# Smaller first groups and later weight loads at the start of a two-branch transformer kernel

## The chip, the cores and the metric

The kernel runs on one core of one Trainium2 chip. The metric is device time in microseconds of the whole program, median of several executions. A profile takes one execution; its times start at the first instruction.

Engine names in the profile: PE is the matmul engine, PEld its weight loads, DVE is VectorE, ACT is ScalarE, POOL is GpSimd, whose queue issues the stores, and SP issues the loads.

## The reference, cut to what matters

```python
x = A_x                                    # (1, 2048, 1024) bf16
xn = _layernorm(x)
return x + _A_ref(xn, ...) + _B_ref(xn, B_w1, B_w2, B_w3, B_w4)

def _B_ref(x, w1, w2, w3, w4):             # ... cut: padding
    h = _gelu(_layernorm(x) @ w1)          # 1024 x 1024
    hs = shifted(h) @ w2                   # four column blocks, shifted by -1, +1, -2, +2 rows
    x1 = x + hs
    return x1 + _gelu(_layernorm(x1) @ w3) @ w4
```

Branch A is an attention over segments; it comes later in the kernel and is not touched. The change is in the first 100 of about 1680 us: `xn`, the second layernorm `xn2`, and `h = gelu(xn2 @ w1)`.

## The kernel before

The rows of x are taken in 16 tiles of 128. `phase0` normalises a tile, stores `xn`, and transposes it on PE in two forms: `xn` through a spread matrix for branch A (`hst`), and `xn2` through the identity (`xn2T`). `stage1` multiplies by w1, four tiles at a time. A scheduler then orders the instructions of each engine into a list, and each engine runs its own list in that order (an instruction that is ready waits behind one that is not).

```python
for n in range(NT):                                          # 16 tiles
    xt = ring.tile([P, D], BF16, tag="xt", bufs=8)
    xts.append(xt)
    nc.sync.dma_start(xt[:], x_v[:, n, :])
    if n == 3:
        nc.sync.dma_start(w1_sb[:], ...)                     # 2 MB
nc.sync.dma_start(w2_sb[:], ...)                             # 2 MB
for k in range(KT):
    nc.sync.dma_start(w3_sb[:, k, :], w3_v[:, k, :])         # 8 x 0.9 MB

def phase0(g):
    hst  = ring2.tile([P, KT, 528], BF16, tag="hst")
    xn2T = ring2.tile([P, KT, 512], BF16, tag="xn2T")
    for j in range(4):
        n = 4 * g + j
        # DVE: bn_stats x2, bn_aggr, small ops; POOL: rr = pow(...)      ... cut
        xn = ring.tile([P, D], BF16, tag="xn")               # the ring has 3 buffers
        nc.vector.tensor_scalar(xn[:], xt[:], ...)
        nc.gpsimd.dma_start(xn_v[:, n, :], xn[:])            # store of xn, 256 KB
        nc.scalar.activation(xn2[:], xt[:], ACTF.Identity, ...)
        # PE: 8 spread matmuls of xn -> hst, copied by DVE (1) and ACT (2)
        # PE: 8 transposes of xn2  -> xn2T, copied by DVE (1) and ACT (1)
    nc.gpsimd.dma_start(hT_d[...], hst[:])                   # 1 MB
    return xn2T

def stage1(g, xn2T):
    for co in range(KT):
        ps = psum.tile([P, 512], F32, tag="mm", bufs=4)
        for k in range(KT):
            nc.tensor.matmul(ps[:], w1_sb[:, k, co*P:(co+1)*P], xn2T[:, k, :], ...)
        nc.scalar.activation(hTB[...], ps[:], ACTF.Gelu_apprx_tanh)

prev = phase0(0)
for g in range(1, 4):
    cur = phase0(g)
    stage1(g - 1, prev)
    prev = cur
stage1(3, prev)
# phase 2 follows: h @ w2, tile by tile
```

Of the kernel before, what the change touches and what calls it, by code (L numbers as in the profile page):

```python
# [13 lines left out]
BF16 = mybir.dt.bfloat16  # L14
F32 = mybir.dt.float32
I32 = mybir.dt.int32
ALU = mybir.AluOpType
ACTF = mybir.ActivationFunctionType
# [3 lines left out]
P = 128  # L22
S = 2048
D = 1024
KT = D // P
# [37 lines left out]
def kernel(  # L63
# [16 lines left out]
    nc = tc.nc  # L80
# [13 lines left out]
    hT_d = tc.dram_tile([P, KT, TH], BF16, name="hT_scratch")  # L94
# [4 lines left out]
    def const_tile(name, arr):  # L99
        d = nc.inline_tensor(_bf(arr), name=name)  # L100
        t = cpool.tile(list(arr.shape), BF16, name=name + "_sb")
        nc.gpsimd.dma_start(t[:], d.ap())
        return t

    spread_np = np.zeros((P, 132), np.float32)
    for t in range(P):
        j, i = divmod(t, SEG)
# [3 lines left out]
    ident = const_tile("c_ident", np.eye(P, dtype=np.float32))  # L111
# [12 lines left out]
    xsum = cpool.tile([P, KT, NSEG], BF16)  # L124
# [46 lines left out]
    with ExitStack() as bctx:  # L171
        psum = bctx.enter_context(tc.tile_pool(name="psum", bufs=2, space=PSUM))
        rctx = bctx.enter_context(ExitStack())
        w3_pool = rctx.enter_context(tc.tile_pool(name="w3", bufs=1, side="right"))
        w3_sb = w3_pool.tile([P, KT, F], BF16)
        w3_v = B_w3.rearrange("(k p) n -> p k n", p=P)
        with ExitStack() as hctx:
            keep = hctx.enter_context(tc.tile_pool(name="keep12", bufs=1))
            hTB = keep.tile([P, KT, S + 4], BF16)
            w2_sb = keep.tile([P, KT, D], BF16)  # L180
# [3 lines left out]
            with ExitStack() as p0:  # L184
                big = p0.enter_context(tc.tile_pool(name="p0big", bufs=1))
                ring = p0.enter_context(tc.tile_pool(name="p0ring", bufs=3))
                ring2 = p0.enter_context(tc.tile_pool(name="p0ring2", bufs=2))
                w1_sb = big.tile([P, KT, D], BF16)
                xts = []
                for n in range(NT):  # L190
                    xt = ring.tile([P, D], BF16, tag="xt", bufs=8)
                    xts.append(xt)
                    nc.sync.dma_start(xt[:], x_v[:, n, :])
                    if n == 3:
                        nc.sync.dma_start(w1_sb[:], B_w1.rearrange("(k p) n -> p k n", p=P))
                nc.sync.dma_start(w2_sb[:], B_w2.rearrange("(k p) n -> p k n", p=P))
                for k in range(KT):
                    nc.sync.dma_start(w3_sb[:, k, :], w3_v[:, k, :])
                def phase0(g):
                    hst = ring2.tile([P, KT, 528], BF16, tag="hst")  # L200
                    xn2T = ring2.tile([P, KT, 512], BF16, tag="xn2T")
                    for j in range(4):
                        n = 4 * g + j
                        xt = xts[n]
                        st = ring.tile([P, 2, 6], F32, tag="st")
                        for c in range(2):
                            nc.vector.bn_stats(st[:, c, :], xt[:, c * 512:(c + 1) * 512])
                        mv = ring.tile([P, 2], F32, tag="mv")
                        nc.vector.bn_aggr(mv[:], st[:])
                        ab = ring.tile([P, 2], F32, tag="ab")  # L210
                        nc.vector.tensor_scalar(ab[:, 0:1], mv[:, 1:2], EPS, None, op0=ALU.add)
                        nc.vector.tensor_scalar(ab[:, 1:2], ab[:, 0:1], EPS, mv[:, 1:2], op0=ALU.mult, op1=ALU.add)
                        rr = ring.tile([P, 2], F32, tag="rr")
                        nc.gpsimd.tensor_tensor(rr[:], ab[:], neghalf[:], op=ALU.pow)
                        nm2 = ring.tile([P, 1], F32, tag="nm2")
                        nc.vector.tensor_scalar(nm2[:], mv[:, 0:1], rr[:, 1:2], -1.0, op0=ALU.mult, op1=ALU.mult)
                        xn = ring.tile([P, D], BF16, tag="xn")
                        nc.vector.tensor_scalar(xn[:], xt[:], mv[:, 0:1], rr[:, 0:1], op0=ALU.subtract, op1=ALU.mult)
                        nc.gpsimd.dma_start(xn_v[:, n, :], xn[:])
                        xn2 = ring.tile([P, D], BF16, tag="xn2")  # L220
                        nc.scalar.activation(xn2[:], xt[:], ACTF.Identity, bias=nm2[:], scale=rr[:, 1:2])
                        for ei, (k0, kn) in enumerate(((0, 3), (3, 3), (6, 2))):
                            ps = psum.tile([P, 3, 132], F32, tag="tr")
                            for k in range(kn):
                                nc.tensor.matmul(ps[:, k, :], xn[:, (k0 + k) * P:(k0 + k + 1) * P], spread[:], start=True, stop=True)
                            if ei == 0:
                                nc.vector.tensor_copy(hst[:, k0:k0 + kn, 132 * j:132 * (j + 1)], ps[:, 0:kn, :])
                            else:
                                nc.scalar.copy(hst[:, k0:k0 + kn, 132 * j:132 * (j + 1)], ps[:, 0:kn, :])
                        for k0 in (0, 4):  # L230
                            ps = psum.tile([P, 4, P], F32, tag="tr")
                            for k in range(4):
                                nc.tensor.matmul(ps[:, k, :], xn2[:, (k0 + k) * P:(k0 + k + 1) * P], ident[:], start=True, stop=True)
                            if k0 == 0:
                                nc.vector.tensor_copy(xn2T[:, k0:k0 + 4, j * P:(j + 1) * P], ps[:])
                            else:
                                nc.scalar.copy(xn2T[:, k0:k0 + 4, j * P:(j + 1) * P], ps[:])
                    nc.gpsimd.dma_start(hT_d[:, :, 7 + 528 * g:7 + 528 * (g + 1)], hst[:])
                    nc.gpsimd.tensor_copy(xsum[:, :, 16 * g:16 * (g + 1)], hst[:].rearrange("p k (s i) -> p k s i", i=33)[:, :, :, 0])
                    return xn2T  # L240

                def stage1(g, xn2T):
                    for co in range(KT):
                        ps = psum.tile([P, 512], F32, tag="mm", bufs=4)
                        for k in range(KT):
                            nc.tensor.matmul(ps[:], w1_sb[:, k, co * P:(co + 1) * P], xn2T[:, k, :], start=(k == 0), stop=(k == KT - 1))  # L246
                        nc.scalar.activation(hTB[:, co, 2 + g * 512:2 + (g + 1) * 512], ps[:], ACTF.Gelu_apprx_tanh)

                prev = phase0(0)
                for g in range(1, 4):  # L250
                    cur = phase0(g)
                    stage1(g - 1, prev)
                    prev = cur
                stage1(3, prev)

            xn3T_pool = rctx.enter_context(tc.tile_pool(name="xn3T", bufs=1, side="right"))
            xn3T = xn3T_pool.tile([P, KT, S], BF16)
            with ExitStack() as p2:
                ring = p2.enter_context(tc.tile_pool(name="p2ring", bufs=4))
                for n in range(NT):  # L260
# [4 lines left out]
                    for ch in range(2):  # L265
                        ps = psum.tile([P, 512], F32, tag="mm", bufs=4)
# [16 lines left out]
                    for k0 in (0, 4):  # L283
                        ps = psum.tile([P, 4, P], F32, tag="tr")
# [4 lines left out]
        with ExitStack() as p3:  # L289
# [7 lines left out]
            for tb in range(4):  # L297
                for f in range(FT):
                    ps = psum.tile([P, 512], F32, tag="mm", bufs=4)
# [11 lines left out]
                for j in range(4):  # L311
                    n = tb * 4 + j
                    R1 = ring.tile([P, D], F32, tag="R1")
                    nc.sync.dma_start(R1[:], R1_v[:, n, :])
                    xt = ring.tile([P, D], BF16, tag="xt")
# [3 lines left out]
                    for ch in range(2):  # L319
                        ps = psum.tile([P, 512], F32, tag="mm", bufs=4)  # L320
# [190 lines left out]
    with tc.If(cond > 0):  # L511
        with ExitStack() as fctx:
# [17 lines left out]
            with tc.For_i(0, NSEG, 1) as i:  # L530
                nc.sync.dma_start(hseg[:, :, M:L], hT_d[:, :, bass.ds(i * 33 + 8, SEG)])
                nc.sync.dma_start(Rt[M:L, :], R_d[bass.ds(i * SEG, SEG), :])
                for hg in range(8):
# [8 lines left out]
                    ps = fps.tile([P, 4, L], F32, tag="mm")  # L542
# [4 lines left out]
                    ps = fps.tile([P, 4, L], F32, tag="mm")  # L547
# [4 lines left out]
                    ps = fps.tile([P, 512], F32, tag="mm")  # L552
# [33 lines left out]
                for ch in range(2):  # L586
                    ps = fps.tile([P, 512], F32, tag="op")
# [47 lines left out]
```

## Time and profile before

1681.85 us, median of four executions (1681.47 to 1682.9).

| what | before | view |
|---|---|---|
| PE busy over the span | 97% | the page, part 1 |
| first stage1 matmul | 26.9 us | timeline |
| first phase 2 matmul | 99.4 us | timeline |
| DMA, 10 to 56 us | saturated, about 400 GB/s | table by stretches |

The busy times of the whole span, from the page:

```profile
PE 1634.8 (97%) x10385; PEld 856.5 (51%) x10385; DVE 647.7 (39%) x1528; ACT 641.8 (38%) x1305; POOL 221.5 (13%) x380
```

PE is the bottleneck nearly everywhere, so time can only be won where PE stands. That is at the start. The table by stretches gives busy microseconds of each engine (with the number of instructions), the granted PE clock (1.00 also where the trace has no clock record), and the busy share and rate of the DMA engines:

```profile
core 0: us, PE busy (x) PEld busy (x) DVE busy (x) ACT busy (x) POOL busy (x), PEclk, DMA share, GB/s
10.20:16.40 6.20, 2.77 (x20) 2.08 (x21) 4.58 (x15) 4.37 (x6) 2.53 (x5) 1.00 1.04 394
16.40:30.00 13.60, 10.05 (x66) 6.80 (x66) 12.16 (x35) 9.35 (x15) 6.49 (x10) 1.00 1.04 404
30.00:56.50 26.50, 23.31 (x175) 13.03 (x173) 21.60 (x64) 20.92 (x35) 10.42 (x16) 1.00 1.02 396
```

Between 16.4 and 30 us PE runs 66 matmuls only. The chain of waits (start, duration, what) shows stage1 starting on a slow PE, and one store of xn that took 13 us:

```profile
26.33 0.82 PE ps L225 x6
27.15 2.13 PE ps L246 x5
29.28 0.16 PE ps L225 x2
29.44 0.43 PE ps L246 x2
...
43.17 13.22 DMA xn_scratch<-xn
```

L246 is stage1, L225 the spread. The first five stage1 matmuls of 512 columns take 0.426 us each, two microseconds later they take 0.216. The timeline (start, duration, engine, line, operation, shapes, number) shows the end of the stage; L269 is phase 2:

```profile
77.40 22.18 PE L246 MATMUL ps<-xn2T,w_sb 128*128 128x512 bf16 x102
99.42 8.15 PE L269 MATMUL ps<-w_sb,hTB 128*128 128x512 bf16 x37
```

Phase 2 follows without a gap. So what the change is worth is read from the start of phase 2.

**PE's busy time is not its work.** Matmuls overlap, and an isolated one shows as longer (a matmul of 512 columns shows as 0.379 us on the average of the profile page, but in a long row one starts every 0.216 us), so below I count work instead: a matmul of N columns counts as N / 2.4 GHz + 2.5 ns. The Trainium skill, "TensorE: Matmul & The Clock Gate", Part 1, gives this as the start-to-start time on a warm PE; this trace agrees (102 matmuls of 512 columns from 77.40 to 99.42 us are 0.216 us each). Stage1 and phase0 together need about 70 us of it. What the clock shows beyond that is *lost* PE time. In the kernel before it is 24.1 us by 30 us (10.2 of them before the first matmul) and 5.0 us more by 70 us. Sums hold to about half a microsecond, since some matmul records are missing from a trace.

### The profile page before, as it was taken

To read this page: it belongs to the slowest core of one execution; us is meant where nothing else is said; L and a number is where in the kernel's file an instruction comes from. 1 tells how busy PE (TensorE), PEld (TensorE's weight loads), DVE (VectorE), ACT (ScalarE), POOL (GpSimd) and SP (SyncE) were. 2 spreads that over 40 slices of the span, in tenths; PEclk is the share of its full clock that TensorE was granted. 3 is DMA by queue.
4 is the path that set the end of the run, shared out by engine and by line. 5 is a ranking of instruction groups with operands and counts; after the bars stand their busy time and mean duration, and the time that the engine had idled before them with its cause. 6 is when DMAs were issued, how large, how long until landed. Compare 5 with 4: busy or idle time off the path is not lost.

```text
span 1679.1 us, 26722 instructions
## 1 busy us (share of the span) xinstructions
PE 1634.8 (97%) x10385; PEld 856.5 (51%) x10385; DVE 647.7 (39%) x1528; ACT 641.8 (38%) x1305; POOL 221.5 (13%) x380
## 2 busy tenths in 40 slices
PE   5999999999999999999999999999999999999998
PEld 3544444444445455554555545554555546665643
DVE  7447000000101145553455505564255533465540
ACT  6635402112030045551455405553255514565520
POOL 4222011010200122210111101110011100101000
PEclk9999999999999999999999999999999999999999
DMA  9544522030309888553556526664365533445211
GB/s 357 225 169 171 188 63 63 31 95 1 100 26 315 313 277 264 169 161 93 171 182 193 165 82 191 181 184 146 116 192 173 179 97 120 137 129 152 65 45 45
DMA packets 202803, 252.93 MB, mean 151 GB/s; under 512 B 15691, under 2 KB 165400, under 8 KB 202672
## 3 DMA queue, kind: packets, MB, share of 16 engines
q1 hardware_dynamic: 186928, 217.25, 41.1%
q0 software_dynamic: 15744, 33.92, 5.8%
q8 instruction: 84, 1.38, 0.4%
q14 instruction: 47, 0.39, 0.1%
HBM read 204.11 MB, written 30.07 MB: 139 GB/s over the span
## 4 chain that ended last, share of the span: by engine, by line
PE 74%; DVE 11%; ACT 5%; DMA 5%; issue 4%; POOL 0%; SPq 0%; DVEq 0%; ACTq 0%; POOLq 0%
PE ps L403 16%; PE ps L415 13%; PE ps L301 11%; PE ps L346 11%; PE ps L322 11%; DVE Pn L463 3%; DVE ss L459 3%; PE psT L467 2%; PE psO L473 2%; ACT e L457 2%; PE psS L450 2%; DVE sm L455 2%; DVE sm L452 2%; DMA wv<-in_A_Wv_dram 1%; PE ps L246 1%
## 5 line engine op out<-in xcount | busy, mean ns | idle before, releaser
L403 PE MATMUL ps<-hTb,wk 128*128 128x396 bf16 (+2 forms) x1536 | 265.7, 313 | 0.0
L403 PE MATMUL ps<-hTb,wq 128*128 128x396 bf16 (+2 forms) x1536 | 263.6, 314 | 0.8 <-DVE Ro L323 0.8
L428 POOL DMA_DIRECT2D V<-Vp x240 | 118.5, 500 | 881.4 <-ACT Vp L416 878.4
L346 PE MATMUL ps<-wo_sb,oX 128*128 128x512 bf16 x1024 | 228.9, 379 | 0.0
L415 PE MATMUL ps<-wv,xTb 128*128 128x512 bf16 x1024 | 227.7, 379 | 0.0
L322 PE MATMUL ps<-w_sb,h3T 128*128 128x512 bf16 x896 | 197.1, 379 | 0.0
L301 PE MATMUL ps<-xn3T,w_sb 128*128 128x512 bf16 x896 | 194.4, 379 | 0.0
L407 ACT ACTIVATE QT<-ps 128x396 bf16<-128x396 f32 (+2 forms) x192 | 87.6, 466 | 255.6 <-PE ps L403 255.6
L452 DVE TENSOR_TENSOR sm<-psS,c_mask_reg_sb 99x396 f32<-99x396 f32 x160 | 87.4, 564 | 217.9 <-PE psS L450 217.9
L403 PEld LDWEIGHTS <-wq 128*128 128x128 bf16 x1536 | 133.6, 98 | 71.3 <-issue 1.1
L302 ACT ACTIVATE h3T<-ps 128x512 bf16<-128x512 f32 x112 | 66.8, 598 | 268.1 <-PE ps L301 268.1
L403 PEld LDWEIGHTS <-wk 128*128 128x128 bf16 x1536 | 131.4, 98 | 67.5
L415 PEld LDWEIGHTS <-xTb 128*128 128x128 bf16 x1024 | 99.8, 98 | 115.8
L346 PEld LDWEIGHTS <-oX 128*128 128x128 bf16 x1024 | 97.8, 98 | 112.2 <-DVE oX L476 1.6
L301 PEld LDWEIGHTS <-w_sb 128*128 128x128 bf16 x896 | 87.6, 98 | 105.2
L322 PEld LDWEIGHTS <-h3T 128*128 128x128 bf16 x896 | 86.9, 98 | 103.1
L323 DVE TENSOR_TENSOR Ro<-ps,R 128x512 f32<-128x512 f32 x32 | 22.1, 691 | 295.6 <-PE ps L322 295.5
L416 ACT CAST Vp<-ps 128x512 bf16<-128x512 f32 x128 | 75.1, 587 | 151.2 <-PE ps L415 147.8
L469 ACT CAST PT<-psT 99x396 bf16<-99x396 f32 (+1 forms) x176 | 86.1, 489 | 62.1 <-PE psT L467 61.1
L405 ACT CAST KT<-ps 128x396 bf16<-128x396 f32 (+2 forms) x192 | 87.7, 457 | 49.1 <-PE ps L403 49.0
L459 DVE TENSOR_REDUCE ss<-e 99x4 f32<-99x396 f32 (+1 forms) x176 | 95.0, 545 | 24.5 <-ACT e L457 23.3
L463 DVE TENSOR_TENSOR Pn<-e,rs 99x396 bf16<-99x396 f32 (+1 forms) x176 | 97.6, 559 | 6.6
(110 smaller groups left out, 1455.3 us busy)
## 6 DMA issues: line engine op xcount, KB each, us to landing
wv<-in_A_Wv_dram SPq DMA_DIRECT2D x48, 1024.0 KB
wq<-in_A_Wq_dram SPq DMA_DIRECT2D x40, 1024.0 KB
wk<-in_A_Wk_dram SPq DMA_DIRECT2D x40, 1024.0 KB
V<-Vp SPq DMA_DIRECT2D x272, 32.0 KB
xt<-in_A_x_dram SPq DMA_DIRECT2D x32, 256.0 KB
R_scratch<-x POOLq DMA_DIRECT2D x16, 512.0 KB, 3.9
R<-R_scratch SPq DMA_DIRECT2D x16, 512.0 KB
R_scratch<-Ro POOLq DMA_DIRECT2D x16, 512.0 KB, 5.0
```

Of the source, the lines that this page charges most:

```text
L301: nc.tensor.matmul(ps[:], w3_sb[:, k, f * P:(f + 1) * P], xn3T[:, k, tb * 512:(tb + 1) * 512], start=(k == 0), stop=(k == KT - 1))
L322: nc.tensor.matmul(ps[:], h3T[:, f, j * P:(j + 1) * P], w4_sb[:, f, ch * 512:(ch + 1) * 512], start=(f == 0), stop=(f == FT - 1))
L346: nc.tensor.matmul(ps[:], oX[:, h, gl * P:(gl + 1) * P], wo_sb[:, h, cc], start=(h == 0), stop=(h == H - 1))
L403: nc.tensor.matmul(ps[:, :nb], w[:, k, hh * P:(hh + 1) * P], B["hTb"][:, k, :nb], start=(k == 0), stop=(k == KT - 1))
L405: nc.scalar.copy(dst[:, hh, :nb], ps[:, :nb])
L407: nc.scalar.mul(dst[:, hh, :nb], ps[:, :nb], scale)
L415: nc.tensor.matmul(ps[:], B["xTb"][:, k, m * P:(m + 1) * P], wv[:, k, :], start=(k == 0), stop=(k == KT - 1))
L428: eng.dma_start(V[r0:r0 + SEG, ti, :], Vp[SEG * (sl % 4):SEG * (sl % 4 + 1), sl // 4, :])
L452: nc.vector.tensor_tensor(sm[:T, :, :T], S3, msk[:].unsqueeze(1).to_broadcast((T, 4, T)), op=ALU.add)
L459: nc.vector.tensor_reduce(ss[:T, :], e[:T, :, :T], axis=AX.X, op=ALU.add)
L463: nc.vector.tensor_tensor(Pn[:T, :, :T], e[:T, :, :T], rs[:T, :].unsqueeze(2).to_broadcast((T, 4, T)), op=ALU.mult)
L469: nc.scalar.copy(PT[:T, :, :T], T3)
```

## The change

Its intent: let stage1 start after one tile rather than four, and keep the 9 MB of w2 and w3, not needed until 100 us and later, out of the way of the loads and stores that the start waits for. It also puts the transposes of xn2 ahead of the spread matmuls.

```diff
-                nc.sync.dma_start(w2_sb[:], ...)
-                for k in range(KT):
-                    nc.sync.dma_start(w3_sb[:, k, :], w3_v[:, k, :])
-                def phase0(g):
-                    xn2T = ring2.tile([P, KT, 512], BF16, tag="xn2T")
-                    for j in range(4):
-                        n = 4 * g + j
+                def phase0(n0, nt):
+                    xn2T = ring2.tile([P, KT, 512], BF16, tag="xn2T", bufs=3)
+                    for jj in range(nt):
+                        n = n0 + jj
 ... (hst is still one buffer for four tiles, stored after the fourth)
-                        nc.scalar.activation(xn2[:], xt[:], ACTF.Identity, ...)
+                        a_xn2 = nc.scalar.activation(xn2[:], xt[:], ACTF.Identity, ...)
+                        if n == 13:
+                            late = [nc.sync.dma_start(w2_sb[:], ...)]
+                            late += [nc.sync.dma_start(w3_sb[:, k, :], ...) for k in range(KT)]
+                            for d in late:
+                                tc.add_manual_dep(d.ins, a_xn2.ins.name, ...)
+                        # transposes of xn2 now first, then the spread matmuls (moved block)
 ...
-                def stage1(g, xn2T):
+                def stage1(n0, nt, xn2T):
+                    w = nt * P
-                            nc.tensor.matmul(ps[:], ..., xn2T[:, k, :], ...)
+                            nc.tensor.matmul(ps[:, :w], ..., xn2T[:, k, :w], ...)
 ...
+                for nt in (1, 1, 2, 4, 4, 4):
+                    groups.append((n0, nt)); n0 += nt
+                # phase0 of a group, then stage1 of the group before it, as before
```

More of the change, by code (lines that the diff above doesn't have):

```diff
@@ L195 @@
                         nc.sync.dma_start(w1_sb[:], B_w1.rearrange("(k p) n -> p k n", p=P))
-                nc.sync.dma_start(w2_sb[:], B_w2.rearrange("(k p) n -> p k n", p=P))
-                for k in range(KT):
-                    nc.sync.dma_start(w3_sb[:, k, :], w3_v[:, k, :])
-                def phase0(g):
-                    hst = ring2.tile([P, KT, 528], BF16, tag="hst")
-                    xn2T = ring2.tile([P, KT, 512], BF16, tag="xn2T")
-                    for j in range(4):
-                        n = 4 * g + j
+                hst_cur = [None]
+                def phase0(n0, nt):
+                    xn2T = ring2.tile([P, KT, 512], BF16, tag="xn2T", bufs=3)
+                    for jj in range(nt):
+                        n = n0 + jj
+                        g, j = divmod(n, 4)
+                        if j == 0:
+                            hst_cur[0] = ring2.tile([P, KT, 528], BF16, tag="hst", name="hst")
+                        hst = hst_cur[0]
                         xt = xts[n]
@@ L220, in phase0 @@
                         xn2 = ring.tile([P, D], BF16, tag="xn2")
-                        nc.scalar.activation(xn2[:], xt[:], ACTF.Identity, bias=nm2[:], scale=rr[:, 1:2])
+                        a_xn2 = nc.scalar.activation(xn2[:], xt[:], ACTF.Identity, bias=nm2[:], scale=rr[:, 1:2])
+                        if n == 13:
+                            late = [nc.sync.dma_start(w2_sb[:], B_w2.rearrange("(k p) n -> p k n", p=P))]
+                            late += [nc.sync.dma_start(w3_sb[:, k, :], w3_v[:, k, :]) for k in range(KT)]
+                            for d in late:
+                                tc.add_manual_dep(d.ins, a_xn2.ins.name, mybir.DependencyInfo(mybir.DependencyClass.Sync, mybir.DependencyReason.DATA),
+                                                  reason="delay bulk weight loads")
+                        for k0 in (0, 4):
+                            ps = psum.tile([P, 4, P], F32, tag="tr")
+                            for k in range(4):
+                                nc.tensor.matmul(ps[:, k, :], xn2[:, (k0 + k) * P:(k0 + k + 1) * P], ident[:], start=True, stop=True)
+                            if k0 == 0:
+                                nc.vector.tensor_copy(xn2T[:, k0:k0 + 4, jj * P:(jj + 1) * P], ps[:])
+                            else:
+                                nc.scalar.copy(xn2T[:, k0:k0 + 4, jj * P:(jj + 1) * P], ps[:])
                         for ei, (k0, kn) in enumerate(((0, 3), (3, 3), (6, 2))):
@@ L229, in phase0 @@
                                 nc.scalar.copy(hst[:, k0:k0 + kn, 132 * j:132 * (j + 1)], ps[:, 0:kn, :])
-                        for k0 in (0, 4):
-                            ps = psum.tile([P, 4, P], F32, tag="tr")
-                            for k in range(4):
-                                nc.tensor.matmul(ps[:, k, :], xn2[:, (k0 + k) * P:(k0 + k + 1) * P], ident[:], start=True, stop=True)
-                            if k0 == 0:
-                                nc.vector.tensor_copy(xn2T[:, k0:k0 + 4, j * P:(j + 1) * P], ps[:])
-                            else:
-                                nc.scalar.copy(xn2T[:, k0:k0 + 4, j * P:(j + 1) * P], ps[:])
-                    nc.gpsimd.dma_start(hT_d[:, :, 7 + 528 * g:7 + 528 * (g + 1)], hst[:])
-                    nc.gpsimd.tensor_copy(xsum[:, :, 16 * g:16 * (g + 1)], hst[:].rearrange("p k (s i) -> p k s i", i=33)[:, :, :, 0])
-                    return xn2T
-                def stage1(g, xn2T):
+                        if j == 3:
+                            nc.gpsimd.dma_start(hT_d[:, :, 7 + 528 * g:7 + 528 * (g + 1)], hst[:])
+                            nc.gpsimd.tensor_copy(xsum[:, :, 16 * g:16 * (g + 1)], hst[:].rearrange("p k (s i) -> p k s i", i=33)[:, :, :, 0])
+                    return xn2T
+                def stage1(n0, nt, xn2T):
+                    w = nt * P
                     for co in range(KT):
@@ L245, in stage1 @@
                         for k in range(KT):
-                            nc.tensor.matmul(ps[:], w1_sb[:, k, co * P:(co + 1) * P], xn2T[:, k, :], start=(k == 0), stop=(k == KT - 1))
-                        nc.scalar.activation(hTB[:, co, 2 + g * 512:2 + (g + 1) * 512], ps[:], ACTF.Gelu_apprx_tanh)
-                prev = phase0(0)
-                for g in range(1, 4):
-                    cur = phase0(g)
-                    stage1(g - 1, prev)
+                            nc.tensor.matmul(ps[:, :w], w1_sb[:, k, co * P:(co + 1) * P], xn2T[:, k, :w], start=(k == 0), stop=(k == KT - 1))
+                        nc.scalar.activation(hTB[:, co, 2 + n0 * P:2 + n0 * P + w], ps[:, :w], ACTF.Gelu_apprx_tanh)
+                groups = []
+                n0 = 0
+                for nt in (1, 1, 2, 4, 4, 4):
+                    groups.append((n0, nt))
+                    n0 += nt
+                prev = None
+                for (n0, nt) in groups:
+                    cur = (n0, nt, phase0(n0, nt))
+                    if prev is not None:
+                        stage1(*prev)
                     prev = cur
-                stage1(3, prev)
+                stage1(*prev)
             xn3T_pool = rctx.enter_context(tc.tile_pool(name="xn3T", bufs=1, side="right"))
```

## The prediction

> **What bounds the kernel now.** The page gives PE 97% busy over 1679.1 us; TensorE works nearly everywhere but at the start, and the change touches only that start (phase0 + stage1). In the timeline stage1's last matmul ends at about 99.4 us and phase 2 follows without a gap, so the gain is how much earlier that moment comes.
>
> Until then PE needs 256 matmuls of 128x512 (102 of them run in 22.0 us, 0.216 us each: 55 us) and 16 tiles of transposes and spreads (in the chain about 0.43 + 0.47 us a tile: 14.5 us), 70 us in all. It takes 99, so about 29 us are lost before 60 us: 10.2 us before the first matmul; 10.2 to 26.9 us, where there are only transposes (VectorE paces a tile at 3.2 us); 26.9 to 41.4 and 47.5 to 59.8 us, where ScalarE, VectorE or late xn stores hold the tiles back. From 59.8 us PE is bound by its own work (36 matmuls, four tiles with 26 between them, then a tail of 102). DMA is saturated (about 400 GB/s) from 5 to 50 us; one xn store took 13.2 us, which with three xn buffers alone allows a tile every 4.4 us.
>
> **What the change does.** w2 and w3 (2 + 7 MB) leave the first 45 us, so that x loads and xn stores get the bandwidth. Groups of 1, 1, 2, 4, 4, 4 tiles let stage1 start at about 12.5 us, once w1 has landed, rather than at 26.9. Matmuls of 128 columns are free on a warm PE: the transposes of 128 columns run at 54 ns, a quarter of 216. The Trainium skill, "TensorE: Matmul & The Clock Gate", Part 1, says that PE runs at half clock until it has been busy for about 3.4 us; the trace agrees (stage1's first matmuls take 0.426 us each, later 0.216), and denser early work should end this by about 20 us instead of 29. The cost is on ScalarE: 16 gelus of 128 columns (estimate 0.25 us) and 8 of 256 (0.38) in place of 8 of 512 (0.60), +2.2 us.
>
> **How much counts.** In the changed order PE has 153 matmuls and four tiles left after tile 11: 33.0 + 3.6 = 36.6 us. Before it had 164, from 59.8 us. Up to tile 11's last copy ScalarE's order holds 15 xn2 (1.2), 12 xn2T (0.55), 12 hst pairs (0.76), 16 + 8 + 4 gelus and one table load (1.28): 44 us, from 9.7 us. At full density tile 11 would be done at 54 us, at 92% (it had about 94% at 27 to 41 us) at 58. So stage1 ends at 58 + 36.6 = 94.5 us, 5 us sooner; VectorE is nearly as full. PE stops being starved, but ScalarE then binds, so only a fifth of the idle time is won. Later stages keep their pace.
>
> **Prediction.** 1677.0 us, 8 in 10 within 1672.5 to 1680.5. Faster by over 2%: 0.005; within 2%: 0.99; slower: 0.005.
>
> **What would show it.** Timeline: first stage1 matmul at 12 to 14 us; PE warm by 20 us; xn stores landing in about 6 us until w2/w3 start at about 48 us; ScalarE about 90% busy from 15 to 57 us; stage1's last matmul near 94.5 us; phase 2 keeping 4.15 us a tile; no wait for w2 or w3.
>
> **What would make it wrong.** If ScalarE and VectorE interlock badly (below 85% density) the gain shrinks to nothing. If their waits vanish, it is up to 10 us. The 9 MB now collide with the last tiles' xn stores, and could stall tiles 14 and 15 for some us. If w1 lands late, PE, which runs in order, blocks in front of it with tile 1 behind.

## The result, and the profile after

1675.71 us, median of 8 runs (1673.51 to 1676.76), against 1681.85 for the kernel before (12 runs). The ratio is 0.9962, 95% interval 0.9952 to 0.9971. (A ratio is the mean time of one kernel's fast runs over that of the other's in the same rounds, so not quite the ratio of the medians. The record lists two more executions of the changed kernel, the profiled one at 1675.5 and one at 1677.35, outside these eight.) The change saves about 6 us. The predicted time was 1677.0 in 1672.5 to 1680.5, so the number was right.

The busy times and the table by stretches after the change:

```profile
PE 1632.0 (98%) x10513; PEld 862.6 (52%) x10513; DVE 646.9 (39%) x1528; ACT 640.6 (38%) x1321; POOL 221.1 (13%) x380
```

```profile
core 0: us, PE busy (x) PEld busy (x) DVE busy (x) ACT busy (x) POOL busy (x), PEclk, DMA share, GB/s
10.20:16.40 6.20, 1.04 (x9) 0.88 (x10) 3.97 (x14) 3.46 (x4) 2.50 (x5) 1.00 1.05 396
16.40:30.00 13.60, 13.39 (x186) 12.64 (x186) 12.46 (x37) 12.76 (x30) 4.61 (x7) 1.00 0.51 178
30.00:56.50 26.50, 24.72 (x233) 17.40 (x231) 23.39 (x67) 23.78 (x47) 13.00 (x21) 1.00 0.60 193
```

Between 16.4 and 30 us PE now runs 186 matmuls (most of them small) where it ran 66, and the DMA engines are half idle. Before 16.4 us it does less than it did. Why is seen in the timeline; L233 is the transposes of xn2, L209 bn_stats, L235 the VectorE half of the copy to xn2T, L241 the spread, L256 stage1:

```profile
10.98 1.03 PE L233 MATMUL ps<-c_ident_sb,xn 128*128 128x128 bf16 x8 [10.98 <-ACT xn L223]
...
13.61 0.69 DVE L209 BATCH_NORM_STATS2 st<-xt 128x6 f32<-128x512 bf16 x1 [2.23 <-DMA xt<-in_A_x_dram]
...
15.67 0.67 DVE L235 CAST xn2T<-ps 128x512 bf16<-128x512 f32 x1
...
16.39 0.49 PE L241 MATMUL ps<-c_spread_sb,xn 128*128 128x132 bf16 x3 [4.38 <-DVE xn2T L235]
...
16.68 0.74 PE L256 MATMUL ps<-xn2T,w_sb 128*128 128x128 bf16 x5
...
17.87 1.81 PE L256 MATMUL ps<-xn2T,w_sb 128*128 128x128 bf16 x15
...
20.43 0.82 PE L256 MATMUL ps<-xn2T,w_sb 128*128 128x128 bf16 x11
```

The transposes of tile 0 are done at about 12 us, but the copy that hands them on stands in VectorE's list behind the statistics of tile 4, whose load queues behind w1. PE waits 4.38 us for it. From 17.87 us fifteen matmuls of 128 columns take 0.107 us each (half clock); from 20.43 us they soon run at 0.056.

```profile
71.88 22.18 PE L256 MATMUL ps<-xn2T,w_sb 128*128 128x512 bf16 x102
93.89 8.15 PE L285 MATMUL ps<-w_sb,hTB 128*128 128x512 bf16 x37
```

Phase 2 (now L285) starts at 93.9 us, 5.5 us sooner; the span is 5.4 us shorter (1679.1 to 1673.7), so in these two traces the later stages neither add nor take.

### The profile page after: what moved, and what is told of

It reads as the page before. It is cut to its first block, busy times and chain, and to the rows that moved or that the text cites. A ratio compares the mean times of both kernels' runs of the same rounds, so it can differ in the third digit from the quotient of the medians.

```text
span 1673.7 us, 26997 instructions
## 1 busy us (share of the span) xinstructions
PE 1632.0 (98%) x10513; PEld 862.6 (52%) x10513; DVE 646.9 (39%) x1528; ACT 640.6 (38%) x1321; POOL 221.1 (13%) x380
## 4 chain that ended last, share of the span: by engine, by line
PE 75%; DVE 10%; ACT 5%; DMA 4%; issue 2%; POOL 0%; SPq 0%; DVEq 0%; ACTq 0%; POOLq 0%
PE ps L419 16%; PE ps L431 13%; PE ps L317 12%; PE ps L362 11%; PE ps L338 11%; DVE Pn L479 3%; DVE ss L475 2%; PE psT L483 2%; PE psO L489 2%; PE ps L256 2%; ACT e L473 2%; PE psS L466 2%; DMA wv<-in_A_Wv_dram 1%; DVE sm L471 1%; DVE sm L468 1%
```

## The experiments

Twelve kernels ran, in three groups of four, each group on one chip beside the kernel before. Every one gave a correct result. The table has for each the time and ratio (where it was timed in rounds), the start of phase 2 from its trace, and lost PE time up to 30 us and from there to 70 us, counted as above.

| kernel | us (runs) | ratio to before | phase 2 starts | lost by 30 us | lost 30 to 70 us |
|---|---|---|---|---|---|
| before | 1681.85 (12) | | 99.4 | 24.1 | 5.0 |
| changed | 1675.71 (8) | 0.9962 | 93.9 | 19.2 | 4.8 |
| delay alone | 1681.98 (5) | 0.9994 | 100.0 | 24.5 | 5.0 |
| groups alone | 1680.98 (5) | 0.9996 | 100.2 | 19.4 | 10.2 |
| groups alone, 6 xn buffers | 1675.47 (5) | 0.9969 | 94.3 | 19.6 | 5.4 |
| before, 6 xn buffers | 1680.86 (1) | | 100.2 | 25.1 | 6.1 |
| changed, more ScalarE work | 1678.33 (1) | | 94.3 | 20.0 | 4.2 |
| changed, more VectorE work | 1675.00 (1) | | 92.2 | 18.8 | 3.8 |
| changed, more PE work | 1680.78 (1) | | 98.9 | 19.3 | 4.5 |
| changed, old transpose order | 1674.30 (5) | 0.9957 | 92.3 | 18.7 | 3.5 |
| changed, x before w1 | 1676.51 (5) | 0.9969 | 94.3 | 19.2 | 4.9 |
| changed, tile 0 copied by ScalarE | 1675.70 (5) | 0.9968 | 93.7 | 20.4 | 3.3 |
| old order, tile 0 copied by ScalarE | 1673.96 (5) | 0.9956 | 92.7 | 19.4 | 3.2 |
| old order, tile 0 by ScalarE, w1 after two tiles | 1678.66 (5) | 0.9990 | 95.4 | 21.5 | 4.4 |

The intervals of the ratios are about plus or minus 0.0014 (2.4 us), so the differences of one or two microseconds between the versions at 1674 to 1676.5 us are not resolved by the times. The trace of the single run with more ScalarE work has a lower mean clock (0.997 against 1.0 for the changed kernel), so its total of 1678.33 is not used; only its start is.

The clock records inside the traces, which no view above prints, show one source of this scatter. In the traces of nine of the twelve kernels PE drops to half clock once or twice more after the start, for 3.41 us each time, at 112 to 120 us or at 627 to 635 us; in those of the kernel before and the changed kernel it does not. Each drop is worth at most 1.7 us (an estimate: half of 3.41). The records also say when PE first leaves half clock: at 29.24 us in the kernel before, 20.51 in the changed one, and up to 3.5 us later in variants of either. A later one costs about half of the delay, so starts of phase 2 that differ by about a microsecond are not told apart by one trace each.

### The two halves of the change, one at a time

The delay alone, with groups of four and the old order:

```diff
-                for nt in (1, 1, 2, 4, 4, 4):
+                for nt in (4, 4, 4, 4):
 # and bufs=3 of xn2T taken back, spread matmuls first again
```

> The kernel before with one part of the change: w2 and w3 issued after the ScalarE pass of tile 13; groups of 4 tiles and the old order of transposes stay. Theory A (late xn stores behind 9 MB of weights held tiles 8 to 11 back, and ScalarE/VectorE bind elsewhere): stage1 ends about 2 us sooner than 99.4 us. Rival B (the gain is the bandwidth alone): about 5 us sooner, near 94. Rival C (the gain is the small groups alone): no change, 99.4.

Measured: phase 2 starts at 100.0 us, the ratio is 0.9994 (interval 0.9981 to 1.0008). No gain. The stores of xn did get fast (median 3.3 us to landing, 6.0 before), and nothing came of it (PE leaves half clock 1.4 us later than in the kernel before, which by the estimate above would account for the 0.6 us). Theory A is wrong about this kernel.

The groups alone, with w2 and w3 issued early again:

```diff
-                        if n == 13:
-                            late = ...
+                nc.sync.dma_start(w2_sb[:], ...)          # ahead of phase0, as before
+                for k in range(KT):
+                    nc.sync.dma_start(w3_sb[:, k, :], w3_v[:, k, :])
```

> The changed kernel with w2 and w3 issued early as before. Theory A: the small groups fill PE from 16 us on, so most of the gain stays: stage1 ends at 95 to 97 us, between the two kernels. Rival B (bandwidth alone): 99. Rival C (groups alone): 94.

Measured: phase 2 starts at 100.2 us, ratio 0.9996 (0.9982 to 1.001). No gain either, so all three theories failed: each half alone is worth nothing, both together 6 us. The table shows how. The groups alone do win the first 30 us (19.4 us lost, as in the changed kernel, not 24.1), and lose them again later (10.2 us, not 4.8). The chain of waits of this run shows where; L223 writes xn, L232 copies to xn2T, L253 is stage1:

```profile
45.95 12.84 DMA xn_scratch<-xn
...
58.88 0.55 DVE xn L223
...
59.55 0.61 DVE xn2T L232
...
61.59 6.74 PE ps L253 x24
```

VectorE waits for a free xn buffer until a store, issued at 45.95 us amid the weights, has landed (the store of tile 10, whose buffer tile 13 needs). It stood 4.78 us for it, and PE 4.05 us. Then comes a second cost, in the table by stretches of the same run:

```profile
58.00:60.00 2.00, 0.00 (x0) 0.00 (x0) 1.12 (x3) 0.00 (x0) 0.27 (x1) 1.00 0.54 220
60.00:62.00 2.00, 1.79 (x13) 1.11 (x13) 1.09 (x3) 0.86 (x3) 0.31 (x1) 0.80 0.37 145
62.00:64.00 2.00, 2.00 (x7) 0.64 (x5) 0.18 (x1) 0.51 (x2) 1.70 (x3) 0.50 0.12 46
64.00:66.00 2.00, 2.00 (x9) 0.83 (x8) 0.00 (x0) 0.60 (x1) 0.05 (x1) 0.84 1.00 348
```

The granted clock falls to 0.50, by the clock records from 61.21 to 64.63 us. The 24 matmuls took 6.74 us in place of 24 x 0.216 = 5.18. This is what "TensorE: Matmul & The Clock Gate", Part 1, of the Trainium skill says: PE goes back to half clock after an idle window of about 3.4 us and needs as long of work to leave it. So the stand of 4 us cost 5.6.

### Is it the bandwidth, or three buffers?

If the weights hurt by holding xn buffers, more buffers should do what the delay does, with the weights left early.

```diff
-                        xn = ring.tile([P, D], BF16, tag="xn")
+                        xn = ring.tile([P, D], BF16, tag="xn", bufs=6)
```

> The small groups with w2 and w3 early, as in the run without the delay, but with six xn buffers rather than three. Theory (the early weights cost their 6 us because VectorE waits for an xn buffer whose store takes 13 us): the wait goes and stage1 ends at 94 to 96 us instead of 100, about 1676 us. Rival (the bandwidth itself is short: x loads and hT stores are late too): 98 to 100, no gain.

Measured: phase 2 at 94.3 us, 1675.47 us, ratio 0.9969 (0.9955 to 0.9982). The stores are no faster: a median of 6.6 us to landing, 6.8 with three buffers. The start of phase 2 (L282) with three buffers, with six, and the view of the stores with six:

```profile
100.17 6.21 PE L282 MATMUL ps<-w_sb,hTB 128*128 128x512 bf16 x28
94.28 1.89 PE L282 MATMUL ps<-w_sb,hTB 128*128 128x512 bf16 x8
DMA to landing us min/median/max: 5.7/6.6/13.5
```

but no instruction waits for them, and the loss after 30 us is 5.4 us, not 10.2. One word in the kernel does what the manual delay of nine loads does. The rival, that bandwidth itself was short, is out.

The same edit on the kernel before:

> The kernel before with six xn buffers. The claim in the prediction that late xn stores held its tiles back says stage1 ends 1 to 3 us sooner than 99.4. Rival (in the kernel before the tiles are early enough, the front is what costs): no change within 0.7 us.

Measured: phase 2 at 100.2 us, no gain. (This is one trace, and PE leaves half clock at 32.08 us in it, 2.8 us later than in the kernel before, so the start of phase 2 alone would not exclude a gain below a microsecond.) The waits say the same more surely: in the trace of the kernel before, VectorE waited 0.2 us in all for a store, in the groups-alone run 6.7 (1.9 before tile 10, 4.8 before tile 13). So in the kernel before, the stores held almost nothing: with groups of four PE falls behind in the first 30 us, and by the time tile 13 is wanted, 56.49 us, its buffer has just come free. The two limits lie one behind the other. Removing the later one shows nothing until the earlier one is gone, and removing the earlier one only brings the work to the later one.

### What binds in the changed kernel after 20 us?

The prediction says ScalarE. ScalarE and VectorE are both busy some 90% from 30 to 56.5 us. To tell, each engine got more work, tiles 0 to 11, with the result unused:

```diff
+                        if n < 12:                          # ScalarE run
+                            junk = ring.tile([P, 512], BF16, tag="junk")
+                            nc.scalar.copy(junk[:], xn2[:, 0:512])
```

```diff
+                        if n < 12:                          # VectorE run
+                            junk = ring.tile([P, 6], F32, tag="junk")
+                            nc.vector.bn_stats(junk[:], xn[:, 0:512])
```

```diff
-                                nc.tensor.matmul(ps[:, k, :], xn2[...], ident[:], start=True, stop=True)
+                                for _ in range(2 if n < 12 else 1):      # PE run
+                                    nc.tensor.matmul(ps[:, k, :], xn2[...], ident[:], start=True, stop=True)
```

> The changed kernel with one more ScalarE copy of 128x512 (about 0.58 us, result unused) for each of tiles 0 to 11, 7 us of ScalarE in all. Theory of the prediction (ScalarE sets the pace from 16 to 56 us): stage1 ends 5 to 7 us later, at 99 to 101 us. Rival 1 (VectorE sets it): under 2 us later. Rival 2 (all engines are near their work and PE most of all): 1 to 4 us later.

> The changed kernel with one more VectorE bn_stats of 128x512 (0.60 us from start to start, result unused) for each of tiles 0 to 11, 7 us of VectorE in all. Rival 1 (VectorE sets the pace): stage1 ends 5 to 7 us later. Theory of the prediction (ScalarE sets it): under 3 us later.

> The changed kernel with each transpose of xn2 run twice for tiles 0 to 11, the second time over the first in the same PSUM tile: 96 more matmuls of 128 columns, 5.3 us of PE at 0.056 us each. New theory (from about 20 us on PE itself is what binds, and ScalarE and VectorE have some us of slack, as 7 us more of either did not move the end of stage1 later): stage1 ends 3.5 to 5.5 us later, at 97.5 to 99.5 us. Theory of the prediction (ScalarE binds and PE waits for it): the extra matmuls fall into PE's waits, under 1.5 us later.

Measured, start of phase 2 against 93.9 us: with about 7 us more on ScalarE 94.3 us; with about 7 us more on VectorE 92.2; with 5.3 us more on PE 98.9, that is 5.0 us later. ScalarE's run (phase 2 is L288), its row of the table by stretches, then the PE run (L286):

```profile
94.33 1.89 PE L288 MATMUL ps<-w_sb,hTB 128*128 128x512 bf16 x8
30.00:56.50 26.50, 25.27 (x244) 18.15 (x242) 23.85 (x68) 26.50 (x54) 12.52 (x20) 1.00 0.56 196
```

```profile
98.90 2.32 PE L286 MATMUL ps<-w_sb,hTB 128*128 128x512 bf16 x10
```

ScalarE could be filled to 26.50 of 26.50 us and phase 2 started 0.4 us later. In the changed kernel it stands idle 6.3 us between 10.2 and 56.5 us (46.3 less 3.46, 12.76 and 23.78). The extra copies filled 2.7 us of that (42.70 busy, not 40.00) and pushed other work of ScalarE past 56.5 us: tile 11's last copy ended 1.5 us later (58.6 us, not 57.1). PE had stage1 matmuls of earlier groups to run meanwhile (it lost 4.2 us from 30 to 70 us, no more than the 4.8 of the changed kernel). So ScalarE does not set the pace, though it is near it; how much more it would take was not tried. On PE nearly every microsecond added comes out at the end (at most 0.9 us of the 5.0 can be the clock: PE leaves half clock at 22.20 us in that run, 1.7 later). The VectorE run is less clean, since the scheduler's new order happened to start stage1 1.5 us sooner (15.2 us); it shows that 7 us more of VectorE does not push the end out, not by how much it is free.

So from about 20 us on, PE is the engine that passes added work on to the end. It is not free of waits: of the changed kernel's 24.0 us lost by 70 us, 17.7 are lost before 20 us (11.0 before any matmul, 4.9 more up to 16.4 us, 1.7 on the cold clock and waits up to 20), and 6.3 after. And the doubled transposes lie on each tile's own way from xn2 to its copy. That a longer way, rather than more work of PE, moved the end is a rival that no run excludes: extra matmuls away from that way were not tried.

### The front

What remains is at the front. Four tries. First, the order of transposes put back:

```diff
 # the block of spread matmuls (xn -> hst) ahead of the block of transposes (xn2 -> xn2T) again
```

> The changed kernel with the spread matmuls ahead of the transposes of xn2 again. Theory: the swap only brings xn2T of tile 0 forward by less than 1 us and is of no weight, stage1 ends at 94 plus or minus 0.7 us. Rival: the swap is what lets the small groups start early, then stage1 ends over 1.5 us later.

Measured: phase 2 at 92.3 us, 1.6 sooner in the trace, 1674.30 us, ratio 0.9957 (0.9943 to 0.9971). Neither expectation was met. The swap is not what helps; if anything it costs a little, which the times do not resolve.

Second, x ahead of w1, so that VectorE would not wait for tile 4:

```diff
-                    if n == 3:
+                    if n == 7:
```

> The changed kernel with w1 queued after the first eight x tiles rather than after four. In the changed kernel VectorE stood until 13.6 us on the load of tile 4, which queues behind w1, with the copy of tile 0's xn2T behind it in its order; PE waited 4.4 us for that copy. Theory: with x first that wait goes and stage1 starts once w1 lands, at about 13.5 us rather than 16.6; the tiles' pace is set by ScalarE and VectorE from there, so stage1 ends about 2 to 3 us sooner, at 91 to 92 us. Rival (the late start is off the path, the pace is set later): no change, 94.

Measured: no gain; stage1 starts at 16.4 us and phase 2 at 94.3. The wait of VectorE is gone, but the scheduler put statistics of later tiles ahead of tile 0's normalisation: its transposes start at 13.23 us, not 10.98, and its copy still comes at 15.43 us. So taking the load away is not enough; what stands before tile 0 in VectorE's list sets the start.

Third, that copy given to ScalarE for tile 0:

```diff
-                            if k0 == 0:
+                            if k0 == 0 and n > 0:
                                 nc.vector.tensor_copy(xn2T[...], ps[:])
```

> The changed kernel with both copies of tile 0's xn2T on ScalarE, so that none stands behind the VectorE pass that waits until 13.6 us for tile 4's load. Theory: stage1 then starts when w1 lands, at 13 to 14 us rather than 16.7, and as the pace after that is near PE's own, stage1 ends 1.5 to 3 us sooner, at 91 to 92.5 us. Rival (the late start is off the path, or w1 itself lands only at 16 us): 94, no change.

Stage1 did start sooner, at 13.10 us, when w1 landed. The timeline shows what became of it (L241 spread, L256 stage1, L243 a VectorE copy of the spread):

```profile
13.10 0.29 PE L256 MATMUL ps<-xn2T,w_sb 128*128 128x128 bf16 x1 [0.28 <-DMA w_sb<-in_B_w_dram]
...
13.51 1.17 PE L256 MATMUL ps<-xn2T,w_sb 128*128 128x128 bf16 x9
18.32 0.38 PE L241 MATMUL ps<-c_spread_sb,xn 128*128 128x132 bf16 x2 [3.64 <-DVE hst L243]
...
19.88 1.59 PE L256 MATMUL ps<-xn2T,w_sb 128*128 128x128 bf16 x13
```

PE ran ten stage1 matmuls and then stood 3.64 us for the next VectorE copy, which is behind the same statistics. The next stage1 matmuls, whose inputs had been there since 13 us, stood behind it in PE's list and ran at 18.49 us. PE is still at half clock at 19.88 us, and by the clock records until 24.05 us, 3.5 us longer than in the changed kernel. Phase 2 starts at 93.7 us, 0.2 sooner. The wait moved, and the slow clock lasted longer.

Both edits together:

> The same edit on the changed kernel with the old order of transposes, which ended stage1 at 92.1 us. If the two gains add: 90 to 91 us and about 1672.5 us in time. If they are the same gain in two forms: 92.

Measured: 92.7 us, 1673.96 us, ratio 0.9956. They do not add.

Last, a try at a faster version, w1 queued after two tiles:

```diff
-                    if n == 3:
+                    if n == 1:
 # on top of the old order and tile 0's copy on ScalarE
```

> A try at a version that beats both: the changed kernel with the old order of transposes, w1 queued after two x tiles and both copies of tile 0's xn2T on ScalarE. If the front (16.4 us before stage1 starts) is still worth something: stage1 starts at 12 us and ends at 89 to 91 us, about 1671 to 1673 us. If tiles then come too slowly to feed PE: stage1 starts sooner and ends at 92, no gain over the old order alone.

It missed: 1678.66 us, stage1 starts at 19.3 us. VectorE's list now has tile 2's statistics ahead of a copy that PE needs, and tile 2 comes behind the 2 MB of w1:

```profile
8.11 0.54 DVE L220 TENSOR_SCALAR xn<-xt,mv,rr 128x1024 bf16<-128x1024 bf16 x1
15.36 0.69 DVE L209 BATCH_NORM_STATS2 st<-xt 128x6 f32<-128x512 bf16 x1 [6.71 <-DMA xt<-in_A_x_dram]
```

No version was found that beats the changed kernel beyond the noise; the two with the old order and w1 in its place measured 1.4 and 1.7 us less.

## Why the prediction was right or wrong, point by point

- **The time and the start of phase 2: right.** 94.5 us was predicted for the end of stage1 and 93.9 measured; 1677.0 us against 1675.71.
- **"PE is bound by its own work" from 59.8 us, 128-column matmuls free, PE warm by about 20 us, later stages keep their pace: right.** The 128-column matmuls ran at 0.056 us once warm; PE was warm soon after 20.43 us.
- **"PE stops being starved, but ScalarE then binds": wrong.** This is the step that failed. I added up ScalarE's work to tile 11 (44 us), divided by 92%, and took the 58 us as its doing. Tile 11's last copy did end at 57.1 us, and 36.8 us of PE followed (36.6 predicted). But ScalarE was busy 40.9 of the 47.4 us from 9.7 us to there, 86%: less work at a lower density, two misses that cancel. It was busy and did not bind: about 7 us more on ScalarE moved phase 2 by 0.4 us, while 5.3 us more on PE moved it by 5.0. PE's own work from 16.7 to 57.1 us, which I did not add up, is 33.4 of 40.4 us, so that no engine's sum alone gives the 58. That the number came out right is here luck.
- **"One xn store took 13.2 us, which with three xn buffers alone allows a tile every 4.4 us", with "late xn stores" among the things that hold the tiles back before: wrong for the kernel before.** Six buffers there gain nothing, and neither does the delay alone. A long store is no wait. The sum itself was sound: once the small groups are in, that limit is the one that binds (groups alone: no gain; with six buffers: the whole gain).
- **"Stage1 to start at about 12.5 us, once w1 has landed": wrong by 4 us.** w1 did land at 13.1 us (in the run where stage1 waited for it), but stage1 started at 16.7, behind a copy in VectorE's list. I had the order of every engine before me and checked PE's and ScalarE's, not VectorE's. But the 4 us were worth little: the run that started at 13.1 us gained 0.2.
- **w2 and w3 at about 48 us:** it was 52.6 us. The fear that they would stall tiles 14 and 15 did not come true: one of the last xn stores took 13.7 us, but nothing waited for it, and PE is busy 9.94 of the 10 us from 62 to 72 us.
- **Cost of small gelus:** 0.25 and 0.38 us estimated, 0.300 and 0.398 measured; off the path.

What stays open: why the old order of transposes ends 1.6 us sooner (the table puts 0.5 us of it before 30 us and 1.3 after), and what the 6.3 us that PE still loses after 20 us hang on. Each edit changes the scheduler's order on all engines at once, and no run isolates it.

## What to carry to other kernels

Two limits in series hide each other: test the parts of a change apart and together, for either alone may show nothing while both are needed. Before calling a busy engine the bottleneck, add up the work of every engine over the same stretch and then give each one some more, away from the path between engines where that can be done; an engine that takes it without moving the end does not bind. A slow store costs nothing until someone wants its buffer back, and then a few more buffers can do what rearranging the traffic does.

## What the Trainium skill lacked or had wrong

- "ScalarE: Activation LUTs", What ACT_TABLE_LOAD costs: it gives about 2.66 us for a switch to another table set (1.28 us of load and 1.38 us of drain). Here the load took 1.28 us and the switch cost 1.31 us in all: in the kernel before it started at 30.96 us, right after a copy, and the gelu began at 32.25; in the changed kernel 18.57 and 19.87. No drain shows in either trace.
- "DMA: Bandwidth & Descriptors", Queues, rings and completion order: it says that the DMA engines take turns between queues packet by packet, and gives no figure for what a store gets beside a bulk load. The trace agrees with the turns: in the groups-alone run, from 43.70 to 58.79 us, the stores' queue moved 626 packets and the loads' queue 628. But these were of 3.6 and 6.3 KB on average, so that the stores got 2.23 MB and the loads 3.97, 148 and 263 GB/s. The xn store of 256 KB issued at 45.95 us took 12.84 us in this, as an hT store of 1056 KB issued at 43.70 landed before it.
- "TensorE: Matmul & The Clock Gate", Part 1: it warns that clock events in a trace are not to be fully trusted. Here they fit the matmuls: the first clock record starts at 29.24 us in the kernel before and at 20.51 in the changed one, just where the matmuls double their pace, and after the stand in the groups-alone run the half clock lasts from 61.21 to 64.63 us, 3.41 us, as the page has it. What misleads is a view: the table by stretches shows 1.00 before the first record, where five matmuls of 512 columns took 2.13 us, half rate.
